# A long convolution and a gated layer on one core: the last spectra in rows 8 partitions apart, two of them moved within SBUF, and a new instruction order

## The chip, the cores and the metric

The kernel runs on one core of a Trainium2 chip. The metric is the device time of one execution in microseconds, taken as the median of several runs. A profile is one more execution, with every instruction and DMA recorded.

## What is computed

```
x   = A_u                                  # [1, 2048, 512] bf16
xn  = layernorm(x)                         # over the 512 channels
K   = Re( C * exp(dt*A*l) * dt*B summed over 128 states ),  l = 0..2047
y   = irfft(rfft(pad(xn)) * rfft(pad(K)))[:2048] + xn * Dskip     # per channel
g,u = xn @ w_gate, xn @ w_up               # 512 -> 1792
out = x + y + (sigmoid(g) * u) @ w_down    # 1792 -> 512
```

## The kernel before

**The gated layer** runs over four groups of 512 tokens. For each group and each of the 14 tiles of 128 hidden channels there is a gate matmul block (L1047, four matmuls of 128x512), an up block (L1071), a sigmoid on ACT (L1059) and a product on DVE (L1086). The product reads the up result from PSUM, or, for the numbers in UEV, from a copy that ACT makes first (L1082). Then come four down-projections of 14 matmuls (L1118), with L1115 to add x through an identity matrix in the last group.

**The convolution** goes by matmuls with constant matrices. The channels are cut in two halves p of 256 and the spectrum in eight units u. `W`, the table of powers of the state matrix that the kernel's taps are made from, comes out of a ladder of eleven levels: ACT squares level k (L712), DVE makes level k+1 (L721, L723), and a Pool DMA casts level k into the table (L717). The f32 levels rotate through three buffers, so the DVE step to level k+1 waits until the cast of level k-2 has landed. Complex products on DVE (L773 to L779) then expand the table, matmuls turn it into the taps, and these are stored to y_scr in DRAM. The input's first transform goes through z_scr. For each half and unit there follow: a load from z_scr and a matmul step (L927), a shuffle (L936), two loads from y_scr and the kernel's spectrum (L955), products on DVE (L962, L966), the inverse's first step (L980), a cast into one of two buffers `vs`, and a store of 256 KB to v_scr. Twelve loads bring v_scr back into the tile `vall` as one table over all units. `VPART` groups them: the first half, the first six units of the second half, and its last two units; each load waits for all stores of its group, and two loads of the last group are on ACT's DMA queue. The last matmuls read `vall`: L1024 for the first three groups (with L1018 to add what is there already), L1010 inside the down-projections of the last group.

**Order.** Nothing is scheduled at run time. Each step is an operation with a number, and the list `ORDER` names the sequence in which they are emitted; each engine runs its own in that order, and buffers are handed out and given back in it. `ON_DVE` names the casts out of PSUM that DVE makes (L329); ACT makes the others (L327). `ON_ACT` names normalisations that ACT makes. All DMAs but Pool's go through one helper (L462), nearly all of them on the SP queue, which waits in order too. L573 is a matmul without a use that keeps PE running.

The last step of the end, as it is issued in the old kernel:

```
lds.append(dma("ACT" if n == 2 and t % 4 else "SP", vall[16 * u0:16 * u1, t // 2, p],
               v_v[:, :, 2 * t:2 * t + 4, :], deps=v_st[n] + table_free + ys_st[1], ...))
```

Of the kernel before, what the change touches and what calls it, by code (L numbers as in the profile page):

```python
# [10 lines left out]
BF = mybir.dt.bfloat16  # L11
F32 = mybir.dt.float32
I32 = mybir.dt.int32
ACT = mybir.ActivationFunctionType
# [9 lines left out]
NT = 16  # L24
# [3 lines left out]
NA, NB = 64, 32  # L28
# [7 lines left out]
NU = 16  # L36
# [41 lines left out]
def _build_S2(by):  # L78
    h = np.zeros((64, 64))
    a = np.arange(64)  # L80
    h[0, :] = 1.0 / 2048
    h[1, :] = (-1.0) ** a / 2048
    for s in range(1, 32):
        h[2 * s, :] = 2.0 / 2048 * np.cos(2 * np.pi * s * a / 64)
        h[2 * s + 1, :] = -2.0 / 2048 * np.sin(2 * np.pi * s * a / 64)
    S2 = np.zeros((128, NA))
    S2[0:64] = h
    S2[64:128, 32:64] = h[:, 0:32]
    return S2.reshape(2, NU, 4, NA).transpose(1, 0, 2, 3)[by].reshape(128, NA)
# [140 lines left out]
def _consts():  # L230
# [17 lines left out]
UEV = (6, 9, 11, 12, 14, 15, 16, 17, 18, 19, 20, 21, 22, 23, 24, 25, 26, 27, 28, 29, 30, 31, 32, 33, 35, 36, 37, 38, 39, 40, 41, 42, 47, 52, 55,)  # L248
ON_DVE = (93, 119, 122, 218, 235, 289, 291, 295, 297, 300, 331, 361, 413, 422, 474, 610, 614, 689, 777, 782, 790, 868, 872, 878,)
ON_ACT = (2, 6, 7, 10, 11, 14, 15)  # L250
ORDER = [
# [110 lines left out]
def kernel(  # L362
# [31 lines left out]
    def two(slot):  # L394
        return pairs[slot.idx][:]
# [54 lines left out]
    VPART = ((0, 0, NU // 2), (1, 0, NU // 2 - 2), (1, NU // 2 - 2, NU // 2))  # L450
    y_scr = [dram.tile([128, NHH, DW], BF, name="y_scr%d" % p) for p in range(NP)]
    v_scr = [dram.tile([4 * (u1 - u0), 128, DW], BF, name="v_scr%d" % n) for n, (p, u0, u1) in enumerate(VPART)]
# [256 lines left out]
    for k in range(11):  # L709
# [5 lines left out]
        def f_cw(cur=cur, k=k):  # L715
            with nc.allow_non_contiguous_dma(reason="laid out"):
                P.dma_start(out=W_all[:, :, k], in_=cur)  # L717
# [67 lines left out]
    for c in range(4):  # L785
# [101 lines left out]
        for n, hr in enumerate((slice(0, 16), slice(16, NHH))):  # L887
            ys_st[p].append(dma("SP", y_scr[p][:, hr, :], ys[p][:, hr, :], deps=y_evs[n], prio=PC, pkt=8192 if n == 0 else 5120, rel=[])
                            (128 * 512 * (16 if n == 0 else NHH - 16)))
# [3 lines left out]
    kgen[3][0].rel += tuple(_Slot(k, i) for k, n, m in (("xx", 3, 4), ("zx", 2, 7)) for i in range(n, m))  # L893
    ys_st[0][-1].rel += tuple(_Slot(k, i) for k, n, m in (("xx", 0, 3), ("pp", 0, 1)) for i in range(n, m))
    ys_st[1][-1].rel += tuple(_Slot("zx", i) for i in range(7, 10))
# [6 lines left out]
                vs=[OFF["kx"] + 4 * KB, OFF["kx"] + 6 * KB], zx=[OFF["zs"], OFF["zs"] + 2 * KB] + [o * KB for o in (14, 20, 22, 28, 30, 4, 6, 12)])  # L902
# [7 lines left out]
    v_st = [[] for _ in VPART]  # L910
    for p in range(NP):
        dsl = slice(DW * p, DW * p + DW)
        for u in UNITS[p]:
# [15 lines left out]
            mm = pl.add("PE", 0.235, fm, [lx, l_m2], QP, acq=[sl], rel=[zsl], mode="Z")  # L929

# [41 lines left out]
            def fv(u=u, sv=sv, pp=pp, pq=pq):  # L972
                for n in range(4):
                    q, y = n % 2, n // 2
                    for g in range(2):
                        ch = slice(DW * g, DW * g + DW)
                        for b in (0, 64):
                            for m in (0, 32):
# [6 lines left out]
            vn = [n for n, (p_, u0, u1) in enumerate(VPART) if p_ == p and u0 <= u < u1][0]  # L985
            vo = 4 * (u - VPART[vn][1])
            v_st[vn].append(dma("SP", v_scr[vn][vo:vo + 4, :, :].rearrange("g q d -> q g d"),
                               lambda vs=vs: vs().rearrange("p g y d -> p (g y) d"), deps=[ev], prio=QP - 1, rel=[vsl],
                               pkt=512)(256 * KB))

    TAIL = dict(ot=OFF["W1"], glu=OFF["W1"] + 4 * KB, xt=OFF["W1"] + 8 * KB)
    vall = at(0, [4, NP, 2, 4, DW])
    vl = []
    for t in range(0, 8, 2):
        lds = []
        for n, (p, u0, u1) in enumerate(VPART):
# [222 lines left out]
```

## Time and profile before

| | us |
|---|---|
| median of 3 runs (lowest, highest) | 232.07 (231.94, 232.74) |
| the profiled execution | 231.0 |
| its span on the core | 228.3 |

| engine | busy us | share of the span |
|---|---|---|
| PE (matmul) | 207.7 | 91% |
| DVE | 196.9 | 86% |
| ACT | 172.1 | 75% |
| POOL | 26.8 | 12% |

The times of instructions come from the profiled execution. An engine's busy share is an average over stages; which engine ended a wait is read from the chain of waits and from the windows. PEclk is the granted clock of TensorE, 1.00 at full speed.

### The profile page before, as it was taken

To read this page: it belongs to the slowest core of one execution; us is meant where nothing else is said; L and a number is where in the kernel's file an instruction comes from. 1 tells how busy PE (TensorE), PEld (TensorE's weight loads), DVE (VectorE), ACT (ScalarE), POOL (GpSimd) and SP (SyncE) were. 2 spreads that over 40 slices of the span, in tenths; PEclk is the share of its full clock that TensorE was granted. 3 is DMA by queue.
4 is the path that set the end of the run, shared out by engine and by line. 5 is a ranking of instruction groups with operands and counts; after the bars stand their busy time and mean duration, and the time that the engine had idled before them with its cause. 6 is when DMAs were issued, how large, how long until landed. Compare 5 with 4: busy or idle time off the path is not lost. (4 is left out here: it accounts for less than half of the span.)

```text
span 228.3 us, 6087 instructions
## 1 busy us (share of the span) xinstructions
PE 207.7 (91%) x2486; PEld 98.4 (43%) x2519; DVE 196.9 (86%) x359; ACT 172.1 (75%) x264; POOL 26.8 (12%) x43
## 2 busy tenths in 40 slices
PE   7899896799999899999999899999998998899694
PEld 2554342244444543553443544464433443444262
DVE  4999693999999999999999999998898999882242
ACT  3899693898998898599999985647799997760020
POOL 2202115253300003504000000003000000000000
PEclk9999999799999999999999999999999999999979
DMA  6999925499844615169957544179986879897974
GB/s 179 357 417 417 182 46 93 89 182 215 215 71 140 142 46 184 52 218 183 296 173 313 148 127 121 34 206 236 289 266 190 220 181 285 240 286 217 236 210 115
DMA packets 50187, 44.61 MB, mean 195 GB/s; under 512 B 9072, under 2 KB 44400, under 8 KB 49776
## 3 DMA queue, kind: packets, MB, share of 16 engines
q1 hardware_dynamic: 46000, 39.44, 57.9%
q0 software_dynamic: 3856, 4.46, 12.2%
q10 hardware_dynamic: 304, 0.33, 0.7%
q8 instruction: 19, 0.31, 0.6%
q14 instruction: 8, 0.07, 0.1%
HBM read 24.30 MB, written 15.47 MB: 174 GB/s over the span
## 5 line engine op out<-in xcount | busy, mean ns | idle before, releaser
L327 ACT ACTIVATE big<-pair 128x1024 bf16<-128x1024 f32 (+2 forms) x78 | 74.5, 994 | 16.5 <-PE pair L927 4.2
L1071 PE MATMUL bank<-xnT,wu_sb 128*128 128x512 bf16 x211 | 53.0, 379 | 3.0 <-DVE hT_sb L1086 1.6
L1118 PE MATMUL bank<-wd_sb,hT_sb 128*128 128x512 bf16 (+1 forms) x230 | 51.5, 375 | 3.7 <-DVE hT_sb L1086 3.0
L1047 PE MATMUL bank<-xnT,wg_sb 128*128 128x512 bf16 (+1 forms) x209 | 49.5, 367 | 2.4 <-issue 0.8
L1118 PEld LDWEIGHTS <-hT_sb 128*128 128x128 bf16 x238 | 22.9, 99 | 29.7 <-DVE hT_sb L1086 4.2
L1047 PEld LDWEIGHTS <-wg_sb 128*128 128x128 bf16 x236 | 21.8, 97 | 25.9 <-issue 4.3
L1071 PEld LDWEIGHTS <-wu_sb 128*128 128x128 bf16 x224 | 20.4, 97 | 28.4 <-issue 7.1
L1059 ACT ACTIVATE hT_sb<-bank 128x512 bf16<-128x512 f32 x52 | 30.0, 623 | 0.4 <-PE bank L1047 0.3
L773 DVE TENSOR_TENSOR big<-big 128x2048 bf16<-128x2048 bf16 (+4 forms) x34 | 28.8, 846 | 0.7 <-DMA big<-big 0.2
L774 DVE TENSOR_TENSOR big<-big 128x2048 bf16<-128x2048 bf16 (+4 forms) x34 | 28.5, 838 | 0.0
L1082 ACT ACTIVATE us_sb<-bank 128x512 bf16<-128x512 f32 x35 | 21.3, 620 | 2.0 <-DVE hT_sb L1086 2.0
L962 DVE TENSOR_TENSOR big<-big 128x2048 bf16<-128x2048 bf16 x16 | 19.5, 1218 | 0.3
L778 DVE TENSOR_TENSOR big<-big 128x1024 bf16<-128x1024 bf16 (+4 forms) x34 | 16.8, 494 | 0.2
L779 DVE TENSOR_TENSOR big<-big 128x1024 bf16<-128x1024 bf16 (+4 forms) x34 | 16.7, 491 | 0.0
L327 ACT ACTIVATE big<-bank 128x512 bf16<-128x512 f32 (+1 forms) x4 | 2.2, 541 | 18.5 <-PE bank L1010 12.9
L329 DVE CAST big<-pair 128x1024 bf16<-128x1024 f32 (+2 forms) x12 | 13.1, 1093 | 3.3 <-PE pair L980 2.4
L712 ACT ACTIVATE big<-big 128x1024 f32<-128x1024 f32 x10 | 10.6, 1056 | 6.5 <-DVE big L723 6.4
L980 PE MATMUL pair<-big 64*32 64x256 bf16 (+1 forms) x512 | 13.3, 324 | 1.5 <-ACT big L327 1.2
L1086 DVE TENSOR_TENSOR hT_sb<-hT_sb,us_sb 128x512 bf16<-128x512 bf16 x35 | 14.2, 416 | 0.2 <-ACT us_sb L1082 0.2
L1086 DVE TENSOR_TENSOR hT_sb<-hT_sb,bank 128x512 bf16<-128x512 bf16 x21 | 13.8, 677 | 0.0
L717 POOL DMA_DIRECT2D big<-big x11 | 8.3, 752 | 33.6 <-DVE big L723 21.4
L721 DVE SCALAR_TENSOR_TENSOR big<-big 128x512 f32<-128x512 f32 x10 | 6.8, 685 | 5.6 <-DMA big<-big 5.6
(93 smaller groups left out, 223.3 us busy)
## 6 DMA issues: line engine op xcount, KB each, us to landing
z_scr<-big SPq DMA_DIRECT2D x16, 256.0 KB
big<-z_scr SPq DMA_DIRECT2D x16, 256.0 KB
v_scr<-big SPq DMA_DIRECT2D x16, 256.0 KB
big<-y_scr SPq DMA_DIRECT2D x32, 104.0 KB
big<-big POOLq DMA_DIRECT2D x11, 256.0 KB, 4.2
big<-in_A_u_dram SPq DMA_DIRECT2D x4, 512.0 KB
y_scr<-big SPq DMA_DIRECT2D x2, 1024.0 KB
big<-v_scr SPq DMA_DIRECT2D x4, 512.0 KB
```

The costliest lines, as they stand in the source:

```text
L327: nc.scalar.activation(out=get(out), in_=get(in_), func=ACT.Identity, scale=1.0 if scale is None else scale)
L773: V.tensor_tensor(out=wide(outp), in0=wide(lo), in1=mre, op=ALU.mult)
L774: V.tensor_tensor(out=wide(tb()), in0=wide(lo), in1=mim, op=ALU.mult)
L778: V.tensor_tensor(out=outp[:, :, 0], in0=outp[:, :, 0], in1=tb()[:, :, 1], op=opr)
L779: V.tensor_tensor(out=outp[:, :, 1], in0=outp[:, :, 1], in1=tb()[:, :, 0], op=opi)
L962: V.tensor_tensor(out=pp().rearrange("p q h m -> p (q h) m"), in0=xx().rearrange("p q h m -> p (q h) m"), in1=kb()[:, 0:2 * DW].unsqueeze( ...
L1047: T.matmul(bank(sl, k % 2)[:, c0:c1], w_at(w, CUT_G, kt, k), xnT[:, grp, kt, c0:c1], start=(kt == 0), stop=(kt == KT - 1))
L1059: S.activation(out=hT_sb[:, hs.idx, k % 2, :], in_=bank(sl), func=ACT.Sigmoid)
L1071: T.matmul(bank(sl), w_at(wu_sb, CUT_U, kt, k), xnT[:, grp, kt, :], start=(kt == 0), stop=(kt == KT - 1))
L1082: S.activation(out=us_sb[:, us.idx, :], in_=bank(sl), func=ACT.Identity)
L1086: V.tensor_tensor(out=h(), in0=h(), in1=us_sb[:, us.idx, :] if on else bank(sl), op=ALU.mult)
L1118: T.matmul(bank(po)[:, 0:c[1] - c[0]], hT_sb[:, hts[k // 2].idx, k % 2, jj * 128:(jj + 1) * 128], wd_sb[:, k, c[0]:c[1]], start=first and ...
```

## The change

1. **Layout and loads of the last spectra.** The rows of the constant S2 are permuted so that unit u owns the partitions u, u+8, ..., u+120 of `vall`. v_scr becomes one tile [2, 8, 4, 128, 256]. A unit's 256 KB are stored as before, and each unit has one load of its own (16 runs of 16 KB), which waits for that unit's store.
2. **Two units without DRAM.** Units 2 and 4 of the second half are not stored. Four DMAs each (64 KB, from `vs` straight into four partitions of `vall`) move them; they wait for all L927 steps, since `vall` lies where their inputs were. All are on SP.
3. **Ladder casts by channel half.** Each L717 DMA becomes two, one for each half p, into the table of that half alone.
4. **The second store of each half to y_scr** waits for the first, and the z_scr buffers have other homes.
5. **A new ORDER**, with other UEV (37 products from ACT's copy, 35 before) and ON_DVE (19 casts on DVE, 24 before). The normalisation of tiles 4 to 8 and five gate and up blocks of the next group come ahead of the ladder and of the first down-projection; casts go out in the order of the levels; the L573 matmuls at the end move to the start.

```diff
-    return S2.reshape(2, NU, 4, NA).transpose(1, 0, 2, 3)[by].reshape(128, NA)
+    return S2.reshape(2, NU, 4, NA).transpose(1, 0, 2, 3)[by].reshape(8, 16, NA).transpose(1, 0, 2).reshape(128, NA)
+DIRECT = ((1, 2), (1, 4))
+VQ = ("SP", "SP", "SP", "SP")
-    VPART = ((0, 0, NU // 2), (1, 0, NU // 2 - 2), (1, NU // 2 - 2, NU // 2))
-    v_scr = [dram.tile([4 * (u1 - u0), 128, DW], BF, name="v_scr%d" % n) for n, (p, u0, u1) in enumerate(VPART)]
+    v_scr = dram.tile([NP, 8, 4, 128, DW], BF, name="v_scr")
...
-                P.dma_start(out=W_all[:, :, k], in_=cur)
+                for p in range(NP):
+                    P.dma_start(out=W[p][:, k], in_=cur[:, p])
...
-            ys_st[p].append(dma("SP", y_scr[p][:, hr, :], ys[p][:, hr, :], deps=y_evs[n], ...
+            ys_st[p].append(dma("SP", y_scr[p][:, hr, :], ys[p][:, hr, :], deps=y_evs[n] + ys_st[p], ...
...
-    vall = at(0, [4, NP, 2, 4, DW])
-            lds.append(dma("ACT" if n == 2 and t % 4 else "SP", vall[16 * u0:16 * u1, t // 2, p], v_v[:, :, 2 * t:2 * t + 4, :],
-                           deps=v_st[n] + table_free + ys_st[1], prio=20 + n + 0.01 * t, pkt=2048, hv=0.9)(64 * KB * (u1 - u0)))
+    vall = at(0, [NP, 2 * NT, DW])
+            if (p, u) in DIRECT:
+                direct.append((p, u, ev, vs, vsl, QP - 1))
+                continue
+    for p, u, ev, vs, vsl, prio in direct:
+        for gy in range(4):
+            vl[p].append(dma(VQ[gy], vall[32 * gy + u:32 * gy + u + 25:8, p], lambda vs=vs, gy=gy: vs()[:, gy // 2, gy % 2, :],
+                             deps=[ev] + fms + table_free + ys_st[1] + (vl[p][-3:] if gy == 3 else []), prio=prio,
+                             rel=[vsl] if gy == 3 else [], pkt=512)(64 * KB))
+    for p, u, st in v_st:
+        vl[p].append(dma("SP", vall[u:u + 121:8, p].rearrange("p i d -> p (i d)"), v_scr[p, u].rearrange("g (q i) d -> (g q) (i d)", i=2 * NT),
+                         deps=[st] + table_free + ys_st[1] + (fms if p else []), prio=20, pkt=16384, hv=0.9)(256 * KB))
```

The lists ORDER, UEV and ON_DVE are exchanged as a whole and are not shown.

More of the change, by code (lines that the diff above doesn't have):

```diff
@@ L247 @@
 SWD = ()
-UEV = (6, 9, 11, 12, 14, 15, 16, 17, 18, 19, 20, 21, 22, 23, 24, 25, 26, 27, 28, 29, 30, 31, 32, 33, 35, 36, 37, 38, 39, 40, 41, 42, 47, 52, 55,)
-ON_DVE = (93, 119, 122, 218, 235, 289, 291, 295, 297, 300, 331, 361, 413, 422, 474, 610, 614, 689, 777, 782, 790, 868, 872, 878,)
+DIRECT = ((1, 2), (1, 4))
+VQ = ("SP", "SP", "SP", "SP")
+UEV = (0, 1, 5, 7, 8, 9, 10, 11, 12, 13, 14, 16, 17, 18, 19, 20, 22, 23, 24, 26, 27, 28, 29, 30, 31, 33, 35, 36, 37, 38, 39, 40, 42, 44, 47, 50, 54,)
+ON_DVE = (93, 94, 95, 96, 119, 218, 235, 287, 292, 294, 297, 301, 318, 348, 387, 396, 697, 798, 876,)
 ON_ACT = (2, 6, 7, 10, 11, 14, 15)
 ORDER = [
[36 rows of a table removed]
[37 rows of a table added]
 class _Op:
@@ L887 @@
         for n, hr in enumerate((slice(0, 16), slice(16, NHH))):
-            ys_st[p].append(dma("SP", y_scr[p][:, hr, :], ys[p][:, hr, :], deps=y_evs[n], prio=PC, pkt=8192 if n == 0 else 5120, rel=[])
+            ys_st[p].append(dma("SP", y_scr[p][:, hr, :], ys[p][:, hr, :], deps=y_evs[n] + ys_st[p], prio=PC, pkt=8192 if n == 0 else 5120, rel=[])
                             (128 * 512 * (16 if n == 0 else NHH - 16)))
@@ L892 @@
     table_free = [x for c in kgen for x in kgen[c]]
-    kgen[3][0].rel += tuple(_Slot(k, i) for k, n, m in (("xx", 3, 4), ("zx", 2, 7)) for i in range(n, m))
+    kgen[3][0].rel += tuple(_Slot(k, i) for k, n, m in (("xx", 3, 4), ("zx", 2, 10)) for i in range(n, m))
     ys_st[0][-1].rel += tuple(_Slot(k, i) for k, n, m in (("xx", 0, 3), ("pp", 0, 1)) for i in range(n, m))
-    ys_st[1][-1].rel += tuple(_Slot("zx", i) for i in range(7, 10))
     l_s2 = load("SP", s2, cten["S2"].ap(), 32 * KB, deps=table_free, pkt=256)
@@ L901 @@
                 pq=[OFF["lad"] + 10 * KB, OFF["pq"]],
-                vs=[OFF["kx"] + 4 * KB, OFF["kx"] + 6 * KB], zx=[OFF["zs"], OFF["zs"] + 2 * KB] + [o * KB for o in (14, 20, 22, 28, 30, 4, 6, 12)])
+                vs=[OFF["kx"] + 4 * KB, OFF["kx"] + 6 * KB], zx=[OFF["zs"], OFF["zs"] + 2 * KB] + [o * KB for o in range(16, 32, 2)])
     mab = at(OFF["lad"] + 6 * KB, [NU, 2, 64])
@@ L908, in slot @@
         return sl, lambda: at(HOME[pool][sl.idx], shape)
-    v_st = [[] for _ in VPART]
+    vall = at(0, [NP, 2 * NT, DW])
+    v_st, fms, vl, direct = [], [], [[], []], []
     for p in range(NP):
@@ L929 @@
             mm = pl.add("PE", 0.235, fm, [lx, l_m2], QP, acq=[sl], rel=[zsl], mode="Z")
+            fms.append(mm)
             ex = pl.copy(nc, 0.91, lambda xx=xx: xx()[:, 0].rearrange("p h (g d) -> p g h d", g=2),
@@ L984 @@
             ev = pl.copy(nc, 0.90, lambda vs=vs: vs().rearrange("p g y d -> p (g y d)"), lambda sv=sv: two(sv), [mv_], QP, acq=[vsl], rel=[sv])
[L985 to L989, printed above, removed]
-    TAIL = dict(ot=OFF["W1"], glu=OFF["W1"] + 4 * KB, xt=OFF["W1"] + 8 * KB)
-    vall = at(0, [4, NP, 2, 4, DW])
[L993 to L996, printed above, removed]
-            v_v = v_scr[n][:].rearrange("g q d -> (g q) d").rearrange("(p j i) d -> p j i d", j=2, i=NT)
-            lds.append(dma("ACT" if n == 2 and t % 4 else "SP", vall[16 * u0:16 * u1, t // 2, p], v_v[:, :, 2 * t:2 * t + 4, :],
-                           deps=v_st[n] + table_free + ys_st[1], prio=20 + n + 0.01 * t, pkt=2048, hv=0.9)(64 * KB * (u1 - u0)))
-        vl.append(lds)
-    vp_op = [vl[t // 2] for t in range(8)]
+            if (p, u) in DIRECT:
+                direct.append((p, u, ev, vs, vsl, QP - 1))
+                continue
+            v_st.append((p, u, dma("SP", v_scr[p, u].rearrange("g q d -> q g d"), lambda vs=vs: vs().rearrange("p g y d -> p (g y) d"), deps=[ev],
+                                   prio=QP - 1, rel=[vsl], pkt=512)(256 * KB)))
+    for p, u, ev, vs, vsl, prio in direct:
[6 more added lines that the diff above has]
+                         deps=[st] + table_free + ys_st[1] + (fms if p else []), prio=20, pkt=16384, hv=0.9)(256 * KB))
+    TAIL = dict(ot=OFF["W1"], glu=OFF["W1"] + 4 * KB, xt=OFF["W1"] + 8 * KB)
     def glu_at(i):
@@ L1009, in s2_mm @@
         for j in range(2):
-            T.matmul(o[64 * j:64 * j + 64, :], s2[:, r, :], vall[:, t // 2, ps, j, 2 * (t % 2) + r, :], start=start, tile_position=(0, 64 * j), **kw)
+            T.matmul(o[64 * j:64 * j + 64, :], s2[:, r, :], vall[:, ps, NT * j + 2 * t + r, :], start=start, tile_position=(0, 64 * j), **kw)
     def final(g, p, gdeps):
@@ L1023, in fy @@
                 for j in range(2):
-                    T.matmul(two(sl)[64 * j:64 * j + 64, DW * q:DW * q + DW], s2[:, q % 2, :], vall[:, g, p, j, q, :], start=False,
+                    T.matmul(two(sl)[64 * j:64 * j + 64, DW * q:DW * q + DW], s2[:, q % 2, :], vall[:, p, NT * j + 4 * g + q, :], start=False,
                              stop=True, tile_position=(0, 64 * j), skip_group_check=True)
-        lds = [x for n, x in enumerate(vl[g]) if VPART[n][0] == p]
+        lds = vl[p]
         my = pl.add("PE", 0.45, fy, lds + [l_s2, mr], 30 + g * 0.01, mode="H")
@@ L1107 @@
             cols = [(0, 256), (256, 512)] if last else [(0, 512)]
-            ver = vp_op[i // 2] + [l_s2]
+            ver = vl[0] + vl[1] + [l_s2]
             def f2(i, po, c, start):
```

73 rows, old and new, of the table ORDER are left out of this document.

## The prediction

> **What bounds the kernel now.** I read the page first: engine totals, then the 40 slices.
>
> ```profile
> PE 207.7 (91%) x2486; PEld 98.4 (43%) x2519; DVE 196.9 (86%) x359; ACT 172.1 (75%) x264; POOL 26.8 (12%) x43
> ...
> PE   7899896799999899999999899999998998899694
> ...
> DVE  4999693999999999999999999998898999882242
> ...
> PEclk9999999799999999999999999999999999999979
> ```
>
> Two engines share the bound. PE works 91% of the span and DVE nearly all of the time between the 8th and the 35th slice. PE loses time in three places only: the first slices, slices 6 and 7, and slice 38, and each of the last two is followed by a slice in which the granted clock falls to 0.7. So a gain must come from there, or from taking work off DVE and PE together. The windows of 10 us put sizes on the first place (PE, PEld, DVE, ACT, POOL busy, clock, DMA share):
>
> ```profile
> 20.00:30.00 10.00, 8.38 (x39) 3.76 (x39) 8.05 (x16) 8.04 (x15) 1.47 (x2) 1.00 0.82 219
> 30.00:40.00 10.00, 8.06 (x37) 3.47 (x36) 6.10 (x13) 6.13 (x13) 3.83 (x7) 1.00 0.51 79
> 40.00:50.00 10.00, 8.86 (x38) 3.32 (x40) 9.67 (x23) 9.23 (x16) 4.35 (x7) 0.83 0.71 129
> 50.00:60.00 10.00, 9.98 (x47) 4.56 (x47) 9.86 (x17) 9.28 (x19) 2.70 (x5) 1.00 1.03 227
> ```
>
> Between 20 and 50 us PE is idle for 4.7 us, and at clock 0.83 it loses another 1.7. The list of waits names the cause, and the wait of DVE is the first link (total us, times, longest):
>
> ```profile
> DVE big L721 <- DMA big<-big: 5.6, 2, 3.8
> ```
>
> DVE's ladder step L721 writes a buffer that the Pool cast (L717) of two levels earlier still reads. It waits twice: 1.85 us at 26.36 and 3.77 us at 39.09. The second is long because cast 3 stands behind cast 4 in Pool's order and waits 3.4 us for DVE's L774. The hidden-layer products L1086 queue behind L721 on DVE, PE's down-projection L1118 waits for them (3.0 us at 38.1), and the up matmuls L1071 wait 1.6 us at 28 to 29 in the same way.
>
> The end is read from the chain of waits, which goes back to the last spectrum:
>
> ```profile
> 204.93 0.82 PE pair L980 x32
> 205.75 0.02 issue
> 205.77 1.24 DVE big L329
> 207.01 0.02 issue
> 207.03 3.90 DMA v_scr<-big
> 210.93 0.03 ACTq L462
> 210.95 0.04 issue
> 210.99 4.83 DMA big<-v_scr
> 215.83 0.04 issue
> 215.87 0.85 PE bank L1010 x4
> ```
>
> The last unit is cast, stored, and loaded back: 10.1 us from the end of its matmuls to the first matmul that uses it. PE had 7.9 us of other work for that time and was idle for 2.17. From 216 to 219 the clock is 0.50 in windows of 1 us: the eight L1024 matmuls take 1.06 us there against 0.63 at 213.07, the two L1018 0.96 against 0.60.
>
> **Which time the sum starts from.** The profiled execution took 231.0 us (span 228.3, 2.7 around it). The median of the runs, 232.07, is 1.07 above it. I sum on 231.0 and add 1.07.
>
> **Part 1, spectra in rows 8 apart, one load a unit.** The store stays (256 KB, 512-byte runs). Twelve loads with 2-KB runs, six of them waiting for the last units' stores, become fourteen loads of sixteen 16-KB runs, each waiting for one store. Before, 1.5 MB of loads ran between 207.4 and 215.8, so the last 128-KB pieces landed 4.83 us after their issue. Afterwards only the last unit's 256 KB comes after the last store. In the trace's packet records a 14,336-byte packet takes 547 ns, so 16 KB about 0.63; the shortest landing of any Pool cast is 3.1 us, and out of an idle queue I estimate 2.4 to 3.0 (outer bounds 2 and 4.8). The last casts are on ACT (1.0 us), not DVE (1.24). From last matmul to first use: 1.0 + 0.15 (the cast of the unit before is ahead of it) + 3.9 + 2.4 to 3.0 = 7.5 to 8.1, against 10.1.
>
> PE's order in that time is: two down-projection blocks of 3.24 us, two L1018 of 0.5 and one L1024 of 0.6, together 8.1. That covers it. The 2.17 us of idle go, and with them the slow clock behind it, for which the pairs above give 0.43 + 0.36 and the eight L1010 between 0 and 1.0; I take 1.2. Sum of the tail: 2.2 + 1.2 = **-3.4 us**, with ends -0.5 (store and load as slow as before) and -4.0. The three L573 matmuls that fill PE behind the last L1118 move to the start; they lay beside the last cast and cost nothing there.
>
> The Trainium skill, page "SBUF — State Buffer", section "Door 1: The DMA port swizzle", says that DMA bandwidth depends on how many of the 16 ports the partitions reach. By its formula rows 8 apart reach eight; by that rule the last load would move its data at half speed, 1.25 us for the 0.63, and the tail would gain 0.6 less at most. No load of this trace has such rows.
>
> **Part 2, two units moved directly.** Units 2 and 4 of the second half are not stored. Each moves by four 64-KB DMAs (128 packets of 512 bytes), all on SP, and only after all sixteen L927 matmuls. It takes 512 KB of store and 512 KB of load off the queues and adds eight issues, less two loads and two stores: net four, at 0.36 to 0.5 us, about 2 us of SP time. Behind them on SP stand a y_scr load of unit 6 and the stores of the last four units (0, 7, 1, 6). A unit holds its vs buffer (there are two) until its fourth DMA lands. So the cast of unit 0 waits for unit 4's, that of unit 7 for unit 2's. After the last L927, PE's order is up block (four matmuls of 0.38), L955 0.41, L980 0.84, gate block 1.5, L955, L980 of unit 0, up block, L980 of unit 7: 7.8 us to the L955 that needs unit 0's buffer of PSUM back. Less the cast's 1.0, unit 4's moves may land 6.8 us after the last L927. Another L955, a block of 3.24 and an L980 later comes the L980 that needs unit 7's: 11.3. Four issues take 1.5 to 2 us, and 512 packets at the 27 ns that a 512-byte packet takes, over 16 engines, 0.9; with a fixed 2 us the four land 4 to 5 us after the last L927, unit 2's 3 to 5 us later. Price nothing while this cover holds; above that, every microsecond counts. One more wait is new: the second y_scr store of a half waits on SP until the first has landed, with the z_scr and y_scr loads behind it. In the old kernel the two of the first half go out at 118.3 and 121.2 and the first load that needs them at 125.7, so a megabyte lands in 4 to 7 us; the wait adds 1 to 4 us to that load. PE's gate and up blocks stand beside it in the order, and I take 0.
>
> **Part 3, ladder casts by halves.** Eleven L717 DMAs become 22 of half the size: 8 us more of Pool issue, and Pool is busy for 12%. A half touches only its own 1 KB of the table, so the order is 0 to 10 and cast 3 no longer waits for L774. That removes the 3.77-us wait or most of it. Each Pool DMA waits for the one eight before it, which is now the cast four levels back, not eight: at landings of 3.1 to 4.2 us this is free, at 8.9 (the first cast, beside the weight loads) it is not. Bounds: 0 to -5.6 us of DVE waiting; I take -4.
>
> **Part 4, the order.** The start has more in front of the ladder: the normalisation of tiles 4 to 8, five gate and up matmul blocks of the next group (4.3 us) ahead of the first down-projection, and the eviction of the second half of xnT, some 1.6 us later by the sums of row durations. Adding up rows on each engine, PE stands 1.2 to 3.4 us behind the old kernel at 29 us. Then it has neither the 1.6 nor the 3.0 us stall, nor the slow clock (1.7): 6.3 us. By the first down-projection (43 us in the old kernel) the sums put PE 0.5 to 1.5 us behind in time but 4.3 us ahead in work, and DVE about 2.5 ahead.
>
> Through the middle both are the bound. DVE's row sum falls from 197.6 to 190.3 us: seven tail casts go to ACT or shrink (4.9, worth nothing in the middle), two L1086 become 416 ns instead of 677, two more normalisations (L588/L589) come. ACT gains 3.3 us of work and is busy 98% in 170 to 190, so it may take the place of DVE there. So 3 to 5 us could be gained up to 150 us. Each stage, however, hands on only what its slowest engine has gained, and the new order's own waits aren't in a sum of rows; of the 3 I keep **-1.0**, with ends +5 (a new stall as long as the two L721 waits) and -5.
>
> **Sum.** 231.0 - 3.4 - 1.0 = 226.6; plus 1.07 is 227.7 us, 1.9% less.
>
> **Rivals.** *The direct moves hold the buffers (slower).* Each has a destination of only four partitions. If four of the 16 engines carry it, each takes 32 packets: 0.9 us a move at 27 ns, 3.2 us at the 101 ns that a packet of the Pool cast takes. Eight moves are then 7 to 26 us where 11.3 are free. At 27 ns nothing is late; from 40 ns on it is; at 70 ns (18 us of moving and 2 fixed) unit 7's cast is some 9 late, and the end is 227.7 + 9 = 236.7. For it: no move within SBUF by SP is in this trace. Against it: the 52-partition loads of y_scr complete in 16 parts each, like all of SP's DMAs. The Trainium skill, page "DMA: Bandwidth & Descriptors", section "Why a DMA increments its semaphore by 16 and not by 1", lets a transfer use the largest number of engines up to 16 that divides the slowest dimension of both sides; for 4 and 128 that is four. A chance of 0.14.
>
> *The early order gives the tail's gain back.* PE is 3.4 behind, and the L721 wait only moves: 231.0 - 3.4 + 3.4 + 1.07 = 232.1, no change. It speaks for it that each half cast now waits on one four levels back. With a full new stall of 4 it is 236. Chances 0.10 and 0.12.
>
> *The whole early gain arrives.* 231.0 - 3.4 - 5 + 1.07 = 223.7: DVE at 9.8 of 10 us in most windows after 50 speaks for it, the ACT load against. 0.14.
>
> *The load is not faster.* Then the tail keeps 10 us against 8.1 of cover: gain 0.5, not 3.4, and 230.6. 0.06.
>
> **How the numbers follow.** The forecast has 0.44 (225.5 to 229.5). About 0.5% (1.2 us) is what a measurement of this kernel can tell from no change. Faster: 0.44 + 0.14 + 0.06 = 0.64; same: 0.10; slower: 0.14 + 0.12 = 0.26. The range 223 to 235.5 leaves out half of the slow cases and the tip of the fast one; the forecast's own is 225.5 to 229.5.
>
> **What would show it.** Right: no DVE L721 wait above 1 us, PE without the hole at 38 to 41 and clock 1.00 in 40 to 50; the last v_scr load landing within 8.1 us of the last L980; no clock below 0.9 after it. Wrong: PE or ACT waiting behind a v cast for a direct move, the moves landing over 5 us after issue, or a hole in PE before 40 us as long as the old one.

## The result, and the profile after

The changed kernel takes 273.18 us (median of 4 runs, 272.22 to 276.02) against 232.41 of the old one beside it: 1.176 times the time (95% interval 1.166 to 1.187). Forecast were 227.7 us and a range to 235.5. The profiled execution has a span of 271.0 us. Ratios, here and below, compare fast runs with fast runs of the old kernel beside them, so a ratio can differ a little from the quotient of two medians.

The page of the changed kernel, engine totals and the 40 slices (6.8 us each here):

```profile
PE 221.1 (82%) x2519; PEld 100.2 (37%) x2519; DVE 192.1 (71%) x354; ACT 177.2 (65%) x271; POOL 36.5 (13%) x54
...
PE   7899889999999999999999999496027932439975
...
DVE  4999799999999999999999588374342902235020
...
PEclk9999999999999999999999999869656996556999
```

Up to the 25th slice (169 us) PE and DVE are as full as before, and the hole that the old kernel has in the seventh and eighth is gone. Then both engines fall to a half and less, together, and TensorE's clock with them. Two engines that are idle together point to a third thing. The list of waits names it (us in total, times, longest):

```profile
ACT big L330 <- DMA big<-v_scr: 21.6, 6, 6.7
DVE big L940 <- DMA big<-v_scr: 15.6, 4, 6.3
ACT big L330 <- DMA big<-big: 15.2, 3, 6.3
DVE big L940 <- DMA big<-big: 8.8, 2, 6.2
```

L330 is ACT's cast out of PSUM (L327 of the old file), L940 the shuffle (L936). Neither reads what a v_scr load or a direct move writes: the casts write the buffers `xx`, `kb` and `vs`, the shuffle reads `xx`, and all of these lie outside the first 32 KB of `big`, where `vall` is. Only a cast into `vs` has a reason to wait for a move, which reads that buffer; the others have none. Yet they wait for these DMAs. The chain shows the other half of it (start, us, what):

```profile
216.55 2.66 DMA big<-big
...
219.31 1.03 ACT big L330
...
220.36 2.58 DMA big<-big
...
223.08 0.73 DVE big L940
...
223.83 2.52 DMA big<-big
...
226.44 1.24 DVE big L966
...
227.74 2.82 DMA big<-big
```

A move lands, a cast starts; the cast ends, the next move starts; it lands, a shuffle starts. All engines and the queue run one behind the other. Seven of the fourteen loads do the same before: between 168.74 and 208.27 the chain has loads of v_scr of 3.1 to 4.6 us each, mostly with single casts and shuffles between them.

Up to that point the early part did what was forecast. The first matmuls of L847 (now L850) start at 72.5 us instead of 76.6, and the first v_scr store goes out at 145.1 instead of 147.7. The windows (PE, PEld, DVE, ACT, POOL, clock, DMA share) show the filled hole and, for contrast, the worst stretch:

```profile
40.00:50.00 10.00, 10.00 (x49) 4.51 (x47) 9.47 (x19) 7.84 (x14) 3.21 (x6) 1.00 0.54 84
...
230.00:240.00 10.00, 3.89 (x52) 1.32 (x59) 2.52 (x3) 1.94 (x2) 0.00 (x0) 0.50 0.06 17
```

### The profile page after: what moved, and what is told of

It reads as the page before. It is cut to its first block, busy times and chain, and to the rows that moved or that the text cites. A ratio compares the mean times of both kernels' runs of the same rounds, so it can differ in the third digit from the quotient of the medians.

```text
span 271.0 us, 6170 instructions
## 1 busy us (share of the span) xinstructions
PE 221.1 (82%) x2519; PEld 100.2 (37%) x2519; DVE 192.1 (71%) x354; ACT 177.2 (65%) x271; POOL 36.5 (13%) x54
## 4 chain that ended last, share of the span: by engine, by line
PE 21%; DMA 17%; DVE 11%; ACT 7%; issue 2%; ACTq 0%; DVEq 0%; SPq 0%
DMA big<-v_scr 9%; PE bank L1119 9%; DMA big<-big 7%; ACT big L330 6%; PE bank L1072 3%; PE bank L1048 2%; DVE big L966 2%; DVE big L940 2%; PE pair L850 2%; DMA big<-z_scr 2%; DVE big L776 1%; PE pair L984 1%; DVE big L777 1%; DVE big L782 1%; DVE big L781 1%
## 5 line engine op out<-in xcount | busy, mean ns | idle before, releaser
L330 ACT ACTIVATE big<-pair 128x1024 bf16<-128x1024 f32 (+2 forms) x79 | 75.8, 1000 | 62.1 <-DMA big<-v_scr 21.6
L1072 PE MATMUL bank<-xnT,wu_sb 128*128 128x512 bf16 x224 | 57.3, 394 | 2.3 <-DVE hT_sb L1087 1.3
L1119 PE MATMUL bank<-wd_sb,hT_sb 128*128 128x512 bf16 (+1 forms) x238 | 54.0, 382 | 1.8 <-DVE hT_sb L1087 1.8
L1048 PE MATMUL bank<-xnT,wg_sb 128*128 128x512 bf16 (+1 forms) x220 | 50.9, 368 | 1.2 <-ACT hT_sb L1060 1.1
L984 PE MATMUL pair<-big 64*32 64x256 bf16 (+1 forms) x512 | 17.6, 396 | 20.2 <-ACT big L330 15.0
L332 DVE CAST big<-pair 128x1024 bf16<-128x1024 f32 (+2 forms) x11 | 11.9, 1084 | 16.2 <-issue 12.0
L984 PEld LDWEIGHTS <-big 64*32 64x32 bf16 x512 | 8.2, 99 | 30.4 <-issue 27.4
L940 DVE LOAD_MASK_SELECT big<-big x16 | 0.2, 14 | 24.5 <-DMA big<-v_scr 15.6
L970 DVE TENSOR_TENSOR big<-big 128x1024 bf16<-128x1024 bf16 x16 | 11.0, 685 | 9.4 <-DMA big<-big 9.4
L720 POOL DMA_DIRECT2D big<-big x22 | 12.1, 552 | 23.4 <-DVE big L726 19.4
L959 PE MATMUL pair<-big 52*32 52x256 bf16 x256 | 7.3, 300 | 8.8 <-ACT big L330 8.5
```

What stands on the lines that cost most here:

```text
L330: nc.scalar.activation(out=get(out), in_=get(in_), func=ACT.Identity, scale=1.0 if scale is None else scale)
L984: T.matmul(two(sv)[o:o + 32, DW * (2 * g + y):2 * DW * (g + 1)], mab[b:b + 64, 2 * u + g, q, m:m + 32], pq()[b:b + 64, q, ch] if y else pp ...
L1048: T.matmul(bank(sl, k % 2)[:, c0:c1], w_at(w, CUT_G, kt, k), xnT[:, grp, kt, c0:c1], start=(kt == 0), stop=(kt == KT - 1))
L1072: T.matmul(bank(sl), w_at(wu_sb, CUT_U, kt, k), xnT[:, grp, kt, :], start=(kt == 0), stop=(kt == KT - 1))
L1119: T.matmul(bank(po)[:, 0:c[1] - c[0]], hT_sb[:, hts[k // 2].idx, k % 2, jj * 128:(jj + 1) * 128], wd_sb[:, k, c[0]:c[1]], start=first and ...
```

## Experiment 1: where the rows lie

The theory after the two traces: a DMA whose destination steps over partitions (`u:u+121:8`) is taken by the build for one that touches the whole range of `big` between its first and its last row. So waits are set between it and accesses of `big` near it in the order. The list of instructions of the built program bears this out. The same cast of ACT and the same shuffle of DVE in the changed kernel and in the kernel `two_tiles` below:

```
changed    L330 Activation big<-pair_63 128x2x2x256 [waits DMAHW5_49,DMAHW6_49,PE_49,Activation_49]
two_tiles  L330 Activation big<-pair_63 128x2x2x256 [waits PE_49,Activation_49]
changed    L940 StreamShuffle big<-big 128x512 [waits DMAHW6_49,DMAHW4_49,DMAHW7_49,DMAHW2_49,DMAHW0_49]
two_tiles  L943 StreamShuffle big<-big 128x512
```

In the changed program 44 instructions of ACT and 24 of DVE wait for a hardware-queue DMA; with the rows of a unit side by side they are 36 and 14, eighteen fewer. The waits go the other way too: 16 of the 22 loads and moves wait for an instruction of ACT or DVE that they do not wait for in two_tiles.

**contiguous_rows**

```diff
-    return ...[by].reshape(8, 16, NA).transpose(1, 0, 2).reshape(128, NA)
+    return ...[by].reshape(128, NA)
-            ... vall[32 * gy + u:32 * gy + u + 25:8, p] ...
+            ... vall[16 * u + 4 * gy:16 * u + 4 * gy + 4, p] ...
-            ... vall[u:u + 121:8, p] ...
+            ... vall[16 * u:16 * u + 16, p] ...
```

> The changed kernel with one thing undone: each unit's sixteen rows of vall lie side by side again (S2 unpermuted, rows 16u to 16u+15), so no DMA has a destination with a partition step. Direct moves, one load a unit, halves, order: as changed. Theory (the stepped destinations make the build add waits between these DMAs and unrelated accesses of the same big tile; 18 waits of ACT and DVE on a DMA go with the step): the two kinds of DMA leave the chain, 25 us of v_scr loads and 18 of direct moves, and the time falls to 226 to 230 us. Rival 1 (direct moves of four partitions are slow in themselves): v_scr loads go, moves stay, 240 us or more. Rival 2 (the new order is slow): over 255 us.

Measured: 250.55 us, ratio 1.077 (1.067 to 1.087). 23 us come back, about half; the 226 to 230 of the theory were missed by 20. The waits for big<-v_scr are gone, but

```profile
ACT big L330 <- DMA big<-big: 11.6, 2, 6.0
```

stays, as in rival 1.

**moves_stepped** and **loads_stepped** put the step back into one kind of DMA each (one line of the diff above).

> As contiguous_rows, but the eight direct moves again go to partitions eight apart (their rows then land where other units' rows belong, so the last spectra are mixed up). Theory: the moves' 18 us on the chain come back, with the waits between them: 244 to 252 us; each move starts only when a cast or a DVE step behind the one before has ended. Rival 1 (only the number of moves or their four partitions matters): the same as contiguous_rows.

> As contiguous_rows, but the fourteen loads of v_scr again go to partitions eight apart (rows then land in other units' places, so the last spectra are mixed up). Theory: their 25 us on the chain come back: 248 to 256 us, with ACT and DVE waiting for big<-v_scr. If the port rule alone slowed the loads (0.6 us each, only the last one seen): within 1 us of contiguous_rows.

Measured, one run each: 261.99 and 259.32 us, 11 and 9 above contiguous_rows. Both lie above the expected ranges, which had been counted from a contiguous_rows of 226 to 230. The waits come back: ACT's casts wait four times for moves in the first kernel, 24.3 us in all, and seven times for loads in the second, 28.0 us. The chain has eight moves in a row of 2.5 to 3.2 us with a cast or DVE step between them in the first, and the loads of 3.1 to 4.9 us in the second. Both costs exist. Their sizes are rough: each is smaller than the share of the changed kernel's chain (18 and 25 us), and since the stepped rows overlap those of the other kind of DMA here, some loads and moves also wait for each other.

**two_tiles** keeps everything of the change, the rows 8 apart too, and takes away only the range in which the build looks:

```diff
-    big = const.tile([128, NBIG // 2], BF, name="big")
+    SPLIT = 39 * KB
+    biga = const.tile([128, SPLIT // 2], BF, name="biga")
+    big = const.tile([128, (NBIG - SPLIT) // 2], BF, name="big")
...
-        v = big[:, off // 2:(off + n) // 2]
+        v = big[:, (off - SPLIT) // 2:(off - SPLIT + n) // 2] if off >= SPLIT else biga[:, off // 2:(off + n) // 2]
```

> The changed kernel, whole, rows 8 apart, with one edit: the SBUF tile big is declared as two tiles (its first 39 KB, where vall lies, and the rest). In the built program the 18 instructions of ACT and DVE that wait for a DMA in the changed kernel and not in contiguous_rows are free of that wait again. Theory (the added waits are the larger part of the loss, and rows 8 apart are the better layout for the DMAs: 16-KB packets of 1.0 us against 1.5): clearly under contiguous_rows, 236 to 244 us. If it also brings the moves to 27 ns a packet, 228 to 234. Rival (it is the rows' distance itself that is slow on the chip): 265 us or more.

Measured: 233.47 us (10 runs, 231.81 to 235.36), ratio 1.004 (0.998 to 1.009). This settles the cause. Of the 17.6% that the change loses, 17.3 go with the added waits; the data, the DMAs, the layout and the order are the same. The theory held; the result is at the end that the expectation tied to packets of 27 ns for the moves, which these are. No cast or shuffle waits for a load any more. What is left of such waits is for the buffers `vs`, which the moves and the stores read:

```profile
ACT big L330 <- DMA biga<-big: 3.4, 2, 2.4
ACT big L330 <- DMA v_scr<-big: 3.3, 2, 3.0
```

It also explains the other half of contiguous_rows. In the built programs ACT and DVE of two_tiles and of contiguous_rows wait for the same hardware-queue DMAs, and the order is the same. The 17 us between these two kernels go with where the rows lie: side by side, a 16-KB packet of the loads takes 1.52 us against 1.03, and a 512-byte packet of the moves 49 ns against 27 (medians). So rows 8 apart are the faster layout, and what they cost in the changed kernel is the waits.

## Experiment 2: the parts that the prediction reckoned with

**old_with_halves** and **old_halves_inorder**: the old kernel with the ladder casts by halves; and that with cast 3 (operation 65) put before cast 4 (68) in ORDER.

```diff
-                P.dma_start(out=W_all[:, :, k], in_=cur)
+                for p in range(NP):
+                    P.dma_start(out=W[p][:, k], in_=cur[:, p])
```

> The old kernel with one thing done: the ladder casts by channel half. By the prediction's part 3 the wait of cast 3 for L774 goes and with it most of the 3.8 us of L721 at 39 us, the hole of PE at 38 to 41 and the slow clock after it: 228 to 231 us. Rival (cast 3 still stands behind cast 4 in Pool's order, and every Pool DMA now waits for the one four levels back): no change, 232, or slower.

> old_with_halves, with cast 3 ahead of cast 4 in Pool's order. If what is left of the L721 wait there (2.6 us) comes from cast 3 standing behind cast 4: another 0.5 to 1.5 us, 227 to 228. If it comes from the first cast's long landing beside the weight loads: no change, 228.4.

Measured: 228.37 us, ratio 0.987 (0.978 to 0.996), and 229.12 us, 0.985 (0.980 to 0.991). The halves alone beat both kernels; the order of the two casts adds nothing that can be told. In the profile of the first, the wait and the window that were 5.6 us and PE 8.86 at clock 0.83:

```profile
DVE big L722 <- DMA big<-big: 2.6, 2, 1.7
```

```profile
40.00:50.00 10.00, 9.90 (x51) 4.16 (x51) 9.90 (x19) 9.83 (x20) 6.02 (x9) 1.00 0.95 159
```

**two_tiles_whole** is two_tiles with the whole casts (the diff above backwards).

> two_tiles with the ladder cast whole (11 DMAs instead of 22). By the prediction's part 3 the halves save up to 4 us of DVE waiting in the old order; here the casts are in the order of the levels in both, but whole casts write a range that spans both halves. Theory: the wait for L777's read comes back, 1 to 4 us slower than two_tiles. Rival: no change.

Measured: 233.36 us, ratio 1.006 (1.001 to 1.010): no different from two_tiles. The expected 1 to 4 us did not come, the rival's "no change" did. In the new order, which has the casts in the order of the levels and the ladder differently mixed, the halves bring nothing that can be told; the ladder step waits 1.7 us for a cast with whole casts, 0.8 with halves.

**no_moves**, **moves_late_loads** and **no_moves_late** are contiguous_rows without moves, with the v_scr loads and the sums of the first half later in the order, and both.

```diff
-        for gy in range(4):
-            vl[p].append(dma(VQ[gy], vall[16 * u + 4 * gy:...], lambda ...: vs()[...], ...
+        st = dma("SP", v_scr[p, u].rearrange("g q d -> q g d"), lambda vs=vs: vs()..., rel=[vsl], ...)
+        vl[p].append(dma("SP", vall[16 * u:16 * u + 16, p]..., v_scr[p, u]..., deps=[st] + ...))
...
 # late: ORDER with 528, 523, ... (loads of the first half) behind 442, the second half's behind 449,
 #       and 792 to 794, 704 to 706 (sums of the first half) behind 448
```

> contiguous_rows without the direct moves: units 2 and 4 of the second half are stored at the place of their first move and loaded like the others, ahead of the first load of a second-half unit. Theory (the moves run on four of the sixteen engines, hold the two vs buffers some 18 us in a row and so cost the two waits of ACT for big<-big, 11.6 us, and the idle PE behind them): 250.5 less 11 to 13 makes 237 to 240 us, and no PE hole at 206 to 212. Rival (the loads that wait for stores at the head of SP's queue hold up the y_scr loads, and that alone makes the 18 us): 246 us or more.

> contiguous_rows with the moves, but the fourteen loads of v_scr stand later in the order: those of the first half behind the last y_scr load, those of the second half behind the last v_scr store; the sums that use the first half (L1019, L1025) move behind the last casts. Theory of the rival: SP no longer waits for a store's landing with y_scr loads behind it (7.2 us at 187 and the holes at 181 to 191), so 243 to 246 us; the moves' waits stay. If only the moves cost: 250 us.

> Both: no moves and the late loads. Theory (the two together are the whole of what contiguous_rows loses against the old kernel, and the early part is 2.5 to 4 us ahead): 228 to 233 us. If it stays over 238, a third cause is in the order of the last third.

Measured: 246.2 us (ratio 1.059, 1.052 to 1.066), 262.34 (1.131, 1.124 to 1.138) and 254.36 (1.096, 1.088 to 1.104). Without the moves 4 us come back, not 11 to 13: the expected size missed, and the time is where its rival, the loads at the head of SP's queue, had it. But the late loads, the test of that rival, missed altogether; they make it 8 to 12 us slower. The loads then come in one bunch: a cast waits 11.7 us for a store beside them in no_moves_late, and 14.4 us for a move in moves_late_loads. In this order early loads, unit by unit, are better.

**moves_by_row** cuts each move of contiguous_rows into four of one partition.

```diff
+                    for b in range(4):
+                        QUEUE["SP"].dma_start(out=vall[16 * u + 4 * gy + b:16 * u + 4 * gy + b + 1, p],
+                                              in_=vs()[32 * b:32 * b + 32, gy // 2, gy % 2, :])
```

> contiguous_rows, but each direct move is cut into four of one partition (32 rows of 512 bytes from 32 partitions): 32 DMAs instead of 8. Theory (a move of four partitions runs on four engines): the packets of 512 bytes now spread over all engines; each unit's moves land within 3 us of their last issue, not 11; SP issues for 6 to 8 us a unit instead, so 245 to 252 us. Rival (the destination's partitions are the limit, not the number of engines): slower than contiguous_rows.

Measured, one run: 256.62 us. The last move lands 2.35 us after its issue. But an issue takes 0.7 us, sixteen of them 11.1 and 10.2 us, and the time is 6 us longer than contiguous_rows, where 245 to 252 was expected.

**new_order_old_loads** has the new order and ladder with the old last part: sixteen stores, twelve loads in three groups; **sums_late** is that with the sums of the first half behind the last casts.

```diff
+SLOTS = (0, 2, 3, 4, 5, 7, 1, 6)
+VPART = ((0, 0, 8), (1, 0, 6), (1, 6, 8))
...
+            vl[p].append(dma("ACT" if n == 2 and t % 2 else "SP", vall[16 * a:16 * b, p, 8 * t:8 * t + 8], v_v[:, 8 * t:8 * t + 8, :],
+                             deps=v_st[n] + table_free + ys_st[1], ...)
```

> The new order and ladder with the old last part: all sixteen units stored, twelve loads with 4-KB runs to 128, 96 or 32 contiguous partitions (units 1 and 6 of the second half, the last in this order, form the last group; two of its loads on ACT's queue), no direct moves. Theory (the whole loss is in the new last part: few-partition loads that occupy all engines, SP held for stores, four-engine moves, stepped destinations; the order and the ladder gained 2.5 to 4 us up to 150 us as forecast): 228 to 231 us, and v_scr stores land in about 4 us again. Rival (the order of the last third loses by itself): 236 us or more.

> new_order_old_loads, with the two sums that use the first half's spectra (L1041, L1047 of groups 2 and 1) moved behind the last v casts, where the old kernel had such work. Theory (what is left of the loss there is PE waiting at those sums for the first half's loads, 4.5 us twice with a slow clock behind): 229 to 232 us, no PE hole at 185 to 192. If the new order loses elsewhere too: 235 us or more.

Measured: 237.30 us (ratio 1.024, 1.013 to 1.034) and 238.45 (1.025, 1.016 to 1.034); both expectations missed, and both times are where the rivals, that the new order loses by itself, had them. In the first the four loads of the first half take 6.81 us in the chain, and PE waits for them at L1047 (that file's line of L1024; the new order has those sums right behind the last store of the first half). In the second the sums are out of the way, and y_scr loads behind the same four loads on SP take their place with 7.59 us. two_tiles, with the same order and one load a unit, is 4 us faster. It fits that the new order needs such loads, but two_tiles differs in the moves and the rows too, so no run shows this alone.

## Experiment 3: why two_tiles is level, and not 2% faster

The chain of two_tiles from its last casts to the first sum that needs the last unit (its file's L1028 is L1024 of the old one; this execution took 235.1 us):

```profile
208.14 1.03 ACT big L330
...
209.19 4.21 DMA v_scr<-big
...
213.50 1.03 ACT big L330
...
214.55 2.31 DMA v_scr<-big
...
216.88 0.47 SPq L467
...
217.80 3.44 DMA out_dram<-glu_sb
...
221.34 0.91 PE pair L1028 x8
```

and the issues of SP in that time:

```profile
210.54 4.38 SPq L467 DMA_DIRECT2D v_scr<-big  x2
215.04 2.31 SPq L467 DMA_DIRECT2D biga<-v_scr  x3
```

The last cast stands at 213.50, 3.0 us late, since its `vs` buffer is held until unit 7's store has landed; that store was late because its cast waited 2.4 us for the moves. The last store lands 2.31 us after its issue, and its load and the start of the matmul take another 4.4. The chain names an output store as the last thing before L1028, but the DMAs that these matmuls wait for in the built program are v_scr loads and moves alone; by the updates of their semaphores the three loads land at 218.5, 219.6 and 221.1. Three loads, 768 KB, stand behind the last store in SP's order: those of unit 7, whose store had landed at 213.4, of unit 1, whose store landed at 214.7, and of unit 6, which lands behind the other two. From the last L987 matmul (210.06) to 221.34 are 11.3 us, with 3.3 of PE idle.

> two_tiles, with the two sums of the first half (L1022, L1028 of groups 2 and 1) behind the last v casts. In two_tiles PE waits 2.0 us at 189 for their loads, has a slow clock (0.83 over 10 us) behind, and is idle 3.3 us at 218 for the last load. Theory (these sums belong in that last gap): 2 to 5 us less, 228 to 231. Rival (PE then waits at 189 for the next thing, since DVE and ACT are the limit there): no change, 233.

> two_tiles without direct moves: the two units are stored and loaded like the others. In two_tiles ACT waits 3.4 us for the moves, and the last cast 3.0 us for a v store. Theory of the forecast (moves cost nothing, they save 1 MB of traffic): the same or up to 2 us slower. Rival (moves hold the vs buffers): 2 to 4 us faster.

> Both edits. If they add up: 226 to 230 us, under both kernels. If the limit is SP's queue or the vs buffers of the last units: 231 to 234.

Their edits to two_tiles are those of the late sums and of no_moves above (loads to rows 8 apart). Measured: 232.54 us (ratio 1.000, 0.996 to 1.004), 231.59 (1.002, 0.997 to 1.008) and 230.49 (0.992, 0.987 to 0.997). Neither edit alone can be told from two_tiles. Both together are 1.2% below it, with intervals that don't meet (each measured beside its own runs of the old kernel), and 0.8% below the old kernel; the expected 226 to 230 was missed by half a microsecond. The moves do not pay: without them, with 1 MB more traffic, it is no slower.

## Why the prediction was wrong, step by step

**The step that failed** is the second sentence of part 1, "fourteen loads of sixteen 16-KB runs, each waiting for one store", and its sibling in part 2, "Price nothing while this cover holds". They count what a DMA waits for by its data. What the build makes of it was not looked at: loads and moves to stepped partitions also wait for casts, shuffles and products, and these for them. two_tiles shows it: with these waits gone, 40 us are gone. The prediction asked who waits for the new DMAs on SP's queue and for the vs buffers, not who waits because of the tile. No rival held this mechanism.

**Part 1, the tail.** 7.5 to 8.1 us were forecast from the last L980 to the first use; two_tiles, free of the added waits, has 11.3, more than the old 10.1. By terms: the cast waits 3.0 us for a buffer (forecast 0.15), the store lands in 2.3 (3.9), the load in 4.4 with the start of the matmul (2.4 to 3.0). "Afterwards only the last unit's 256 KB comes after the last store" does not hold: three loads do. A 16-KB packet takes 1.03 us in the packet records of this kernel (0.63 forecast). The gain of 3.4 us did not come.

**Part 2 and its rival.** The rival's mechanism was there. In two_tiles, while moves alone run, the DMA share is:

```profile
199.00:201.00 2.00, 1.95 (x59) 0.92 (x52) 2.00 (x3) 2.00 (x3) 0.00 (x0) 1.00 0.28 83
```

0.28 of sixteen engines are 4.5, with packets of 27 ns (median): the rival's lower end. Unit 4's four moves free their buffer 5.6 us after the last L927 and unit 2's 10.7, inside the 6.8 and 11.3 that were reckoned as free for PE, and PE idles only 0.8 and 0.5 us behind the two casts. But ACT is ready 0.9 and 2.4 us before the buffers, so the casts are that late, and with them the stores, which hold the buffer that the last cast waits for. That path was not priced. So "at 27 ns nothing is late" was right for PE alone. With contiguous rows, where the same packets take longer (49 ns in the median between 205 and 213 us), casts waited 11.6 us for the moves. The rule of the Trainium skill, page "DMA: Bandwidth & Descriptors", section "Why a DMA increments its semaphore by 16 and not by 1", gives four engines here, and the trace agrees: besides the 4.5 busy, a move updates its semaphore once early and four times when it lands. The argument against it, "complete in 16 parts each", was a misreading: in the old kernel's trace a 52-partition load of y_scr makes 14 updates, one early and 13 when it lands.

**Part 3** was right in size for the old order: -4 us of waiting forecast, 5.6 to 2.6 us measured, and 3 to 4 us of time. The sum has no term of its own for it; it is in the 6.3 us of part 4. In the new order the halves bring nothing that can be told.

**Part 4** was right in the early part: PE without the hole, clock 1.00 from 40 to 50 us, 4.1 us ahead at 72.5 us and 2.6 at the first v_scr store, more than the 1.0 that the sum kept. The new order then gives it back: sums of the first half are placed where their loads have not landed (2.0 us of PE at 189 and a clock of 0.83 in 190 to 200 in two_tiles), and the buffer wait of the tail follows. That two_tiles_no_moves_late, with the late sums and no moves, is faster than both kernels agrees with this; what each of the two gives by itself stayed below what these runs can tell. The term put at nothing for the second y_scr store, which waits for the first, no run takes out alone. Two small misreadings carry nothing: the hole of the old PE line is in its seventh and eighth slices, not 6 and 7, and behind the store at 207.0 seven loads of together 1.6 MB were issued, not 1.5.

## What to carry to other kernels

Before pricing a DMA by its queue and its data, read in the built program which instructions wait for it: one destination with a partition step inside a large shared tile can tie together engines that have nothing to do with it. If such a layout is wanted, give its region a tile of its own. And test the parts one by one: here one line of the old kernel was worth 1.3% alone, and the whole change lost 17.6%.

## What the runs showed of the hardware

- **Rows 8 apart do load faster.** A 16-KB packet of the v_scr loads takes 1.02 us (median) with rows 8 apart in the changed kernel, 1.03 in two_tiles, and 1.52 with sixteen rows side by side in contiguous_rows. The Trainium skill, page "SBUF — State Buffer", section "Door 1: The DMA port swizzle", gives eight ports to the first and, by its formula, four to the second; the trace agrees in direction, with a factor of 1.5, not 2. A 2-KB packet of the old loads takes 84 ns, an eighth of the size in a twelfth of the time.
- **Moves of four partitions** keep 4.5 of the sixteen DMA engines busy in two_tiles, with 27 ns for a 512-byte packet. **Moves of one partition** are bound by their issue, 0.7 us each; while they run the DMA engines are hardly busy (share 0.12):

```profile
203.00:211.00 8.00, 3.16 (x86) 1.38 (x85) 5.53 (x9) 1.95 (x3) 0.00 (x0) 0.95 0.12 25
```

- **Where PE is idle again and again, the granted clock stays low.** From 230 to 240 us of the changed kernel PE is busy 39% and the clock is 0.50 throughout, so the lost overlap costs twice: first the wait, then the matmuls behind it at half speed (32 L984 take 1.48 us at 204.87, with a clock of 0.50 from 204 to 207, and 0.84 at 212.61 with 1.00).
